# Expert 0's early rows moved from the first expert stage into the attention's plan, and expert 2's weights put behind the first transposes

## The chip, the cores and the metric

The kernel runs as one program on one core of a Trainium2 chip. The metric is the device time of one execution in microseconds (us). The engines are PE (TensorE, with PEld its weight loads), DVE (VectorE), ACT (ScalarE), POOL (GpSimd) and SP (SyncE, used here for DMA issues alone).

## The reference

Three stages follow each other; each takes the output of the one before.

```python
# 1: attention, 4 x 8 heads, 768 tokens, head size 48; one state (48x48) per head
y[t] = q[t] @ state
v_old = state^T k_n[t];  state += beta[t] * outer(k_n[t], v[t] - v_old)

# 2: x is (3072, 384); eight experts, each token to one of them
logits = x @ w_gate;  e_idx = argmax(logits);  probs = softmax(logits)
eom = sigmoid(x @ w_output_gate)
for e in range(8):
    rows = e_idx == e
    out[rows] = probs[rows, e] * eom[rows, e] * (relu(x[rows] @ w1[e]) @ w2[e])   # 384 -> 1024 -> 384

# 3: four experts, every token through all of them
p = domain_probs / domain_probs.sum(-1)
out = sum over e of p[:, e] * (relu(x @ w1[e]) @ w2[e])
```

## The kernel before

**Number formats.** Weights and rows are split into two f16 halves (a high part, and what is left, "lo"); one product is three f16 matmuls (high x high, high x lo, lo x high). One layer over a block of rows is 72 matmuls of 128x128 by as many columns as there are rows: 8 groups of 9 in the first layer (384 to 1024), 3 groups of 24 in the second (1024 to 384). Each group ends with two evictions: ACT writes the high half (L789, in the second layer L801), DVE the lo half (L790, L802).

**Stages.** Attention and routing come first (to about 311 us). The tokens are worked off in 12 chain steps of 64 tokens per sequence (L410); behind each step the finished tokens are transposed (L529, evicted to xT by ACT, L255), multiplied with both gates (L536), written to a table `xd` in DRAM, and counted by expert with prefix sums (L554, L570) into `run` and `acc`. After step 8, `early` (L587 to L600) takes the first 192 rows (EW) of experts 0 and 1 that are known by then, gathers them from `xd` by indirect DMAs into GZ, normalises them (`norm`, L578 to L583) and transposes them by DMA into `xe[0]` and `xe[1]`. `weights` loads the weights of experts 0 (into the buffer kq) and 1 (wa, wb) meanwhile. When all tokens are through, `counts` copies the counts and the row lists into `wid`.

The second stage, `moe1`, then works on windows of rows, one call of `window_` each: the early 192 rows of expert 0 (L787 with xe, L799), those of expert 1, the 240 other rows of expert 0, the 240 of expert 1, then 432 rows for each of experts 2 to 7. `fetch` gets what a window needs: indirect gathers on POOL (L774, xg<-xd,wid; four column buffers of 128 rows), `norm` through two buffers xh, transposes by DMA on SP (L732, xt<-xh; two buffers xt), and for experts 2 to 7 the weights, in seven DMAs on SP through three staging tiles s (L732), split into halves by ACT and DVE (L738, L739). Expert 2's weights go to the buffers w. Results go to `x2` in DRAM by three DMAs of POOL (L805, x<-y), one per 128 of the 384 outputs. `put` (L866, L867, eld<-EL) writes the scales of the rows. Rows beyond 432 of an expert are handled by a general loop that doesn't run here; the arithmetic that finds out (`spill`, recorded as L208) is strewn between.

The third stage, `moe2` (L928, L947), runs from 537.8 us to the end.

**What sets the order.** `Plan` simulates the engines: each operation has an engine, a modelled duration, what it reads and writes, and a priority (smaller is sooner); an engine takes the ready operation with the smallest priority, urgent ones (chain, evictions) first. The instructions are then issued in that order, so each engine runs a fixed list. Attention and routing are one plan, with four PSUM banks as a pool (`Lazy` takes one when the plan runs an operation with `take`); `moe1` is a second plan, with banks of its own, whose instructions all follow those of the first on each engine. Chain step n has priority n, so 20 comes behind all chain steps.

Of the kernel before, what the change touches and what calls it, by code (L numbers as in the profile page):

```python
# [72 lines left out]
STB = 3  # L73
XW = 408
# [408 lines left out]
class Router:  # L483

    NXR=4
    def __init__(self,ctx,tc,dp):
        self.tc=tc; self.nc=tc.nc; self.xd=dp.tile([N,XW],F32,name="xd"); self.eld=dp.tile([N+512,MW],F32,name="eld"); self.ord=dp.tile([NE*N+512,1],I32,name="ord")
# [109 lines left out]
    def weights(self,x):  # L597

        at=self.at; nc=self.nc; st=[(a,[('stw',j)]) for j,a in enumerate(at.stw)]; i=0; h=2*KD*FF
        for e,w,t in (((0,0,self.kq[:,0:h]),(0,1,self.kq[:,h:])),((1,0,self.wa),(1,1,self.wb)))[x]:  # L600
            kc=([('kqT',3-w,x,y) for x in range(2) for y in range(2)]+[('GQ',2,x,1-w) for x in range(2)]) if e else []; at.op('G',1,lambda: None,(),kc+[('Wc',e,w)],'claim')
            n,f,m=((KD,FF,512),(KF,DM,DM))[w]
            src=self.ahead[w][e].rearrange("(n p) f -> p n f",p=128); t=t.rearrange("p (l n f) -> p l n f",l=2,n=n); g=f"wl {2*e+w}"
            for a in range(n):
                for x in range(0,f,m):
                    s,ks=st[i%2]; i+=1; s=s[:,0:m]; at.prio=WPR; h_,l_=(t[:,j,a,x:x+m] for j in range(2)); k=[('W',e,w,a,x)]
                    at.dma(s,src[:,a,x:x+m],(),ks,g,xfer=m*1.42,q=WQ); at.prio=WPR+0.5
                    at.act(100+.833*m,h_,s,ks+[('Wc',e,w)],k,g,scale=64.0)
                    at.op(WLE,70+1.042*m,lambda s=s,h_=h_,l_=l_: nc.vector.scalar_tensor_tensor(out=l_,in0=s,scalar=64.0,in1=h_,op0=ALU.mult,op1=ALU.subtract),ks+k,[('W2',e,w,a,x)],g)
    def counts(self):  # L610
# [100 lines left out]
class Moe:  # L711
# [3 lines left out]
    def __init__(self,ctx,tc,r,w1,w2,v1,v2,out):  # L715
# [26 lines left out]
    def weight(self,t,key,src,n,width):  # L742
# [103 lines left out]
    def moe1(self):  # L846
        nc=self.nc; tc=self.tc; r=self.r; pl=self.pl=Plan(tc,HOP); self.si=self.xi=self.bi=self.ci=self.hi=self.yi=0; self.pp_=0; self.parts={}
        with ExitStack() as c:
# [22 lines left out]
            for e in range(NE):  # L871
# [116 lines left out]
def deltanet_moe(tc,q,k,v,beta,wg,wo,w1,w2,probs,v1,v2,out):  # L988
    nc=tc.nc
    with ExitStack() as ctx:  # L990
        dp=ctx.enter_context(tc.tile_pool(name="dp",bufs=1,space=DRAM))
        r=Router(ctx,tc,dp)
        with ExitStack() as c2:
# [3 lines left out]
            at.ahead=r.weights; r.setup(c2,at,plan,wg,wo,probs); r.ahead=(w1,w2); at.run(); r.counts()  # L997
# [31 lines left out]
```

## Time and profile before

| | us |
|---|---|
| Median of 3 runs | 1254.89 |
| Lowest and highest | 1251.54, 1254.93 |
| The profiled execution, its own time | 1257.36 |
| Its span | 1255.8 |
| PE busy in the span | 1179.4 (94%) |
| DVE, ACT, POOL busy | 781.1, 618.7, 640.4 |

The span is what the profiler recorded between the first and the last instruction; the execution's own time is 1.6 us more, and times of runs are to be compared with the own time. A share of busy time is a mean over stages with different limits, so the windows of the section of rows show the stretches around the change apart. A timeline row is a run of like instructions on an engine: when the first started, from there to the end of the last, how many there were (x), and in brackets the idle time of the engine ahead of it with what ended it; the rows of a longer question join differently from those of a shorter one. "SPq" or "POOLq" marks the DMA queue of an engine.

### The profile page before, as it was taken

Reading aid. Unit: us, or ns where it says so; the run is one execution under the profiler, and the core shown is the slowest. Engines: PE = TensorE matmul, PEld = TensorE weight load, DVE = VectorE, ACT = ScalarE, POOL = GpSimd, SP = SyncE. Lnnn points to the kernel's source line nnn. Section 1 sums busy time; section 2 is a strip of 40 time slices with the busy share of each in tenths; the row PEclk is TensorE's granted clock in tenths of the full one; section 3 lists DMA queues with packets and bytes.
Section 4 is the critical chain, followed back from the end, with each engine's and each line's share of the span. In section 5 each row is a group of like instructions: output and inputs, shape, how many; then the busy total and the mean of one; then the engine's idle time right before and its main releaser. Section 6 shows DMA issues by size and latency. Waiting matters only on the chain.

```text
span 1255.8 us, 38782 instructions
## 1 busy us (share of the span) xinstructions
PE 1179.4 (94%) x16595; PEld 1031.4 (82%) x16595; DVE 781.1 (62%) x1583; ACT 618.7 (49%) x1129; POOL 640.4 (51%) x896
## 2 busy tenths in 40 slices
PE   6988888877989999999999999999999999999997
PEld 5877777766974555589999999999999999999997
DVE  3766837664777787236666566677565776555555
ACT  4546664543545655235445444454444454444442
POOL 9643431442474350055665454576444675566565
PEclk9889998886999999999999999999999999999999
DMA  8445442324779976021111111111111220111101
GB/s 137 84 94 121 97 98 45 98 74 110 182 176 233 244 184 175 29 67 39 40 39 39 35 43 44 48 51 39 34 44 50 65 64 28 37 54 52 52 27 39
DMA packets 151457, 100.74 MB, mean 80 GB/s; under 512 B 107696, under 2 KB 140432, under 8 KB 151280
## 3 DMA queue, kind: packets, MB, share of 16 engines
q1 hardware_dynamic: 133520, 69.18, 22.4%
q0 software_dynamic: 9216, 23.50, 6.7%
q10 hardware_dynamic: 8544, 5.53, 1.5%
q8 instruction: 131, 2.15, 0.7%
q14 instruction: 46, 0.38, 0.1%
HBM read 77.09 MB, written 15.77 MB: 74 GB/s over the span
## 4 chain that ended last, share of the span: by engine, by line
PE 56%; DVE 0%; issue 0%; POOL 0%; ACT 0%; POOLq 0%
PE b L928 30%; PE b L947 26%; POOL out_dram L966 0%; DVE h L940 0%; DVE cc L958 0%; DVE wa L962 0%; DVE sm L958 0%; ACT h L939 0%; ACT a L930 0%; POOL sep L965 0%; POOLq L1024 0%; POOLq L966 0%
## 5 line engine op out<-in xcount | busy, mean ns | idle before, releaser
L928 PE MATMUL b<-wb,v 128*128 128x256 f16 x3456 | 392.6, 273 | 0.4 <-PEq L895 0.4
L928 PEld LDWEIGHTS <-v 128*128 128x128 f16 x3456 | 336.7, 98 | 37.8 <-issue 0.8
L947 PE MATMUL b<-v,h 128*128 128x192 f16 x4032 | 348.2, 246 | 0.0
L947 PEld LDWEIGHTS <-h 128*128 128x128 f16 x4032 | 335.5, 98 | 2.4 <-DVE h L940 0.2
L936 POOL TENSOR_TENSOR S<-a 128x256 f32<-128x256 f32 x192 | 150.8, 804 | 249.8 <-ACT a L930 249.5
L940 DVE TENSOR_TENSOR h<-a,h 128x768 f16<-128x768 f32 x96 | 132.6, 1381 | 134.8 <-ACT h L939 126.5
L940 DVE TENSOR_TENSOR h<-S,h 128x1024 f16<-128x1024 f32 x96 | 117.7, 1226 | 125.8 <-ACT h L939 125.6
L930 ACT ACTIVATE a<-b 128x512 f32<-128x512 f32 x192 | 113.8, 595 | 151.2 <-PE b L928 149.1
L939 ACT ACTIVATE h<-S 128x1024 f16<-128x1024 f32 x96 | 101.4, 1056 | 161.7 <-POOL S L936 142.1
L936 POOL TENSOR_TENSOR S<-S,a 128x256 f32<-128x256 f32 x96 | 126.9, 1322 | 0.0
L939 ACT ACTIVATE h<-a 128x768 f16<-128x768 f32 x96 | 80.9, 843 | 3.0
L936 POOL TENSOR_TENSOR S<-a,S 128x256 f32<-128x256 f32 x96 | 77.0, 802 | 7.2
L958 DVE TENSOR_TENSOR cc<-b,sm 128x192 f32<-128x192 f32 x192 | 58.5, 345 | 2.4 <-ACT sm L952 2.4
L789 ACT ACTIVATE h<-b 128x432 f16<-128x432 f32 (+2 forms) x80 | 35.7, 454 | 40.3 <-PE b L787 36.3
L805 POOL DMA_DIRECT2D x<-y x27 | 19.3, 721 | 68.9 <-DVE y L802 60.8
L790 DVE SCALAR_TENSOR_TENSOR h<-b,h 128x432 f16<-128x432 f32 (+2 forms) x80 | 40.7, 511 | 17.5 <-ACT h L789 17.1
L774 POOL DMA_INDIRECT xg<-xd,wid x28 | 30.2, 1077 | 38.7 <-DVE xh L583 22.0
L958 DVE TENSOR_TENSOR sm<-b,sm 128x192 f32<-128x192 f32 x144 | 46.2, 348 | 1.5
L799 PE MATMUL b<-h,kq 128*128 128x432 f16 (+2 forms) x288 | 42.4, 304 | 4.8 <-DVE h L790 4.8
L787 PE MATMUL b<-xt,w 128*128 128x432 f16 x216 | 42.1, 355 | 2.5 <-DVE wa L739 2.0
L739 DVE SCALAR_TENSOR_TENSOR v<-s,v 128x512 f16<-128x512 f32 (+2 forms) x56 | 41.6, 761 | 4.1 <-ACT v L738 3.9
L267 POOL DMA_DIRECT2D stw<-in_moe_w_dram x28 | 16.0, 571 | 52.6 <-DVE X L374 19.9
(279 smaller groups left out, 1748.0 us busy)
## 6 DMA issues: line engine op xcount, KB each, us to landing
wb<-x SPq DMA_DIRECT2D x72, 256.0 KB, 3.2
s<-in_moe_w_dram SPq DMA_DIRECT2D x40, 384.0 KB, 4.2
s<-in_moe_w_dram SPq DMA_DIRECT2D x18, 512.0 KB, 4.3
s<-in_moe_w_dram SPq DMA_DIRECT2D x24, 256.0 KB, 4.7
xd<-ys ACTq DMA_DIRECT2D x24, 192.0 KB, 3.1
x<-y POOLq DMA_DIRECT2D x18, 216.0 KB, 4.2
stw<-in_moe_w_dram POOLq DMA_DIRECT2D x12, 256.0 KB, 4.0
stw<-in_moe_w_dram POOLq DMA_DIRECT2D x16, 192.0 KB, 3.5
```

The costliest lines, as they stand in the source:

```text
L739: self.op('V',(150+1.042*n)*self.slow,lambda: self.nc.vector.scalar_tensor_tensor(out=lo,in0=s,scalar=64.0,in1=hi,op0=ALU.mult,op1=ALU.sub ...
L787: nc.tensor.matmul(out=ps,lhsT=w1[:,a,k,f*128:(f+1)*128],rhs=xt[:,b*KD+k],start=i==0,stop=i==8); i+=1
L789: self.op('A',160+.85*n,lambda ps=ps,h=h: nc.scalar.activation(out=h[:,0],in_=ps,func=AF.Relu),[('p1',pi)],[('h',hi,0)],**U)
L790: self.op('V',150+1.042*n,lambda ps=ps,h=h: nc.vector.scalar_tensor_tensor(out=h[:,1],in0=ps,scalar=0.0,in1=h[:,0],op0=ALU.max,op1=ALU.sub ...
L799: nc.tensor.matmul(out=ps,lhsT=w2[:,a,f,d*128:(d+1)*128],rhs=hs[f][0][:,b],start=(f,i)==(0,0),stop=(f,i)==(KF-1,2))
L928: for c,y in PASS: nc.tensor.matmul(out=F[k][:,f],lhsT=w[:,c,d,c_:c_+128],rhs=self.xk[B%2][d][:,y,256*i:256*i+256],start=(f,z)==(0,0),stop ...
L930: self.op('A',620,lambda k=k,g=g: A.activation(out=a[ja][:,g].rearrange("p x t -> p (x t)"),in_=F[k].rearrange("p a t -> p (a t)"),func=AF ...
L936: self.op('G',930,lambda o=o,x=x,y=y,w=w: G.tensor_tensor(out=X[o],in0=X[x],in1=X[y],op=w),ka,[ks])
L939: self.op('A',200+.833*m,lambda h=h,q=q,g=g: A.activation(out=h[:,0,:,q],in_=g,func=AF.Copy),kg,[kh+(0,)])
L940: self.op('V',1400 if m==768 else 1350,lambda h=h,q=q,g=g: V.tensor_tensor(out=h[:,1,:,q],in0=g,in1=h[:,0,:,q],op=ALU.subtract),kg+[kh+(0, ...
L947: for z,(c,d) in enumerate(PASS): nc.tensor.matmul(out=Q[k][:,o,0:192],lhsT=h[:,c,g,x],rhs=w[:,d,m,y],start=(m,o,z)==(0,0,0),stop=(m,z)==( ...
L958: self.op('V',340,lambda o=o,k=k,y=y,x=x: V.tensor_tensor(out=o,in0=Q[k][:,y,0:192],in1=s[:,x],op=ALU.add),[(qk,k),('sm',z,x)],[ko])
```

## The change

`Router.window(e)` is new. It is called once, for expert 0, ahead of `counts`, and so puts the early 192 rows of expert 0 through both layers inside the attention's plan, at priority 20 (EPR): the same 72 + 72 matmuls (L624 and L633 in the changed kernel), 11 evictions on ACT (L626, L635), 11 on DVE, and three DMAs on POOL to x2. Its h and y tiles lie in the buffers GQ of steps 3 and 4, its banks come from the pool of four. To write x2 there, its DRAM tiles are made in the router. In `moe1` the call of `window_` for these rows goes. And the weight DMAs of expert 2 now name the first transposed block, `('xt',0,0)`, as something they read, so the plan issues them no sooner than that is there. Behind the new function all line numbers are 28 larger, above it 2 larger.

```diff
--- before.py
+++ after.py
@@ -71,6 +71,8 @@
 AQ = 480
 XLO = 'V'
 STB = 3
+EPR = 20
+LTK = ('xt', 0, 0)
 XW = 408
 MW = 24
 RMQ = 'D'
@@ -484,7 +486,7 @@
 
     NXR=4
     def __init__(self,ctx,tc,dp):
-        self.tc=tc; self.nc=tc.nc; self.xd=dp.tile([N,XW],F32,name="xd"); self.eld=dp.tile([N+512,MW],F32,name="eld"); self.ord=dp.tile([NE*N+512,1],I32,name="ord")
+        self.tc=tc; self.nc=tc.nc; self.xd=dp.tile([N,XW],F32,name="xd"); self.eld=dp.tile([N+512,MW],F32,name="eld"); self.x2=[dp.tile([128,2,N+WIN],F16,name=f"x2{k}") for k in range(KD)]; self.ord=dp.tile([NE*N+512,1],I32,name="ord")
         c=self.c=ctx.enter_context(tc.tile_pool(name="rc",bufs=1)); T=lambda n,s,d=F32: c.tile(s,d,name=n)
         self.wgo=T("wgo",[128,KD,16])
         self.tri=T("tri",[128,128],F16); self.ones16=T("ones16",[128,128],F16)
@@ -607,6 +609,32 @@
                     at.dma(s,src[:,a,x:x+m],(),ks,g,xfer=m*1.42,q=WQ); at.prio=WPR+0.5
                     at.act(100+.833*m,h_,s,ks+[('Wc',e,w)],k,g,scale=64.0)
                     at.op(WLE,70+1.042*m,lambda s=s,h_=h_,l_=l_: nc.vector.scalar_tensor_tensor(out=l_,in0=s,scalar=64.0,in1=h_,op0=ALU.mult,op1=ALU.subtract),ks+k,[('W2',e,w,a,x)],g)
+    def window(self,e):
+
+        at=self.at; nc=self.nc; n=EW; t=f"ew {e}"; at.prio=EPR+0.1*e; w=[x.rearrange("p (l n f) -> p l n f",l=2,n=m) for x,m in zip(((self.kq[:,0:2*KD*FF],self.kq[:,2*KD*FF:]),(self.wa,self.wb))[e],(KD,KF))]
+        kw=[[(z,e,0,a,x) for z in ('W','W2') for a in range(KD) for x in range(0,FF,512)],[(z,e,1,a,0) for z in ('W','W2') for a in range(KF)]]
+        U=[x.rearrange("p h i -> p (h i)").bitcast(F16)[:,2*n*j:2*n*j+2*n].rearrange("p (a t) -> p a t",a=2) for i in (3,4) for x in at.GQ[i] for j in range(5)]; free=lambda s: [('GQ',3+s//10,hh,s//5%2) for hh in range(2)]
+        hs=U[0:8] if e==0 else U[8:16]; y0=16; s0=8*e; x=self.xe[e]; kx=[('xe',e,j) for j in range(2)]
+        def lo(q,k,o,reads,wr,give,op0,sc): at.op('V',150+1.042*n,lambda: nc.vector.scalar_tensor_tensor(out=o[:,1],in0=q(),scalar=sc,in1=o[:,0],op0=op0,op1=ALU.subtract),reads,wr,t,give=give)
+        for f in range(KF):
+            k=('ep',e,f); P=Lazy(at,k); h=hs[f]; kh=('eh',e,f)
+            def mm(P=P,f=f):
+                i=0
+                for d in range(KD):
+                    for a,b in ((0,0),(0,1),(1,0)): nc.tensor.matmul(out=P[:,0:n],lhsT=w[0][:,a,d,f*128:f*128+128],rhs=x[:,b*KD+d],start=i==0,stop=i==8); i+=1
+            at.op('P',9*(n/2.4+3),mm,kx+kw[0],[k],t,take=[k],lat=LP,ni=18)
+            at.op('A',160+.85*n,lambda P=P,h=h: nc.scalar.activation(out=h[:,0],in_=P[:,0:n],func=AF.Relu),[k],[kh+(0,)],t,after=free(s0+f))
+            lo(lambda P=P: P[:,0:n],k,h,[k,kh+(0,)],[kh+(1,)],[k],ALU.max,0.0)
+        for d in range(KD):
+            k=('eq',e,d); P=Lazy(at,k); y=U[y0+d]; ky=('ey',e,d)
+            for f0 in range(0,KF,2):
+                def mm(P=P,d=d,f0=f0):
+                    for f in (f0,f0+1):
+                        for i,(a,b) in enumerate(((0,0),(0,1),(1,0))): nc.tensor.matmul(out=P[:,0:n],lhsT=w[1][:,a,f,d*128:d*128+128],rhs=hs[f][:,b],start=(f,i)==(0,0),stop=(f,i)==(KF-1,2))
+                at.op('P',6*(n/2.4+3),mm,[('eh',e,f,j) for f in (f0,f0+1) for j in range(2)]+kw[1],[k],t,take=[k] if f0==0 else (),lat=LP,ni=12)
+            at.op('A',160+.85*n,lambda P=P,y=y: nc.scalar.activation(out=y[:,0],in_=P[:,0:n],func=AF.Copy,scale=2.0**-8),[k],[ky+(0,)],t,after=free(y0+d))
+            lo(lambda P=P: P[:,0:n],k,y,[k,ky+(0,)],[ky+(1,)],[k],ALU.mult,2.0**-8)
+            at.dma(self.x2[d][:,:,0:n],y,[ky+(0,),ky+(1,)],[('x2',d)],t,xfer=n*2,q='G')
     def counts(self):
         at=self.at; nc=self.nc; cp=Lazy(at,'wcnt')
         at.op('P',60,lambda: nc.tensor.matmul(out=cp[:,0:8],lhsT=self.ones16,rhs=self.run,start=True,stop=True),['run','rc'],['wcnt'],"cnt",take=['wcnt'])
@@ -721,9 +749,9 @@
 
         a=[t.bitcast(F32).rearrange("p (j d) -> p j d",d=DM) for t in (r.kq,r.wa)]; self.acc=lambda j: a[j//16][:,j%16]
         w=r.wb; self.xk=[[w[:,1024*(KD*i+k):1024*(KD*i+k)+1024].rearrange("p (y t) -> p y t",y=2) for k in range(KD)] for i in range(2)]
-        self.x2=[self.dp.tile([128,2,N+WIN],F16,name=f"x2{k}") for k in range(KD)]
+        self.x2=r.x2
         pp=ctx.enter_context(tc.tile_pool(name="pp",bufs=1,space=PSUM)); self.bank=[pp.tile([128,512],F32,name=f"b{i}") for i in range(8)]
-    gate=(); slow=1.0
+    gate=(); slow=1.0; late=()
     def op(self,e,dur,fn,reads=(),writes=(),**k):
         k.setdefault('prio',self.prio); self.pl.add(e,dur,fn,reads,writes,**k)
     def dma(self,out,in_,reads,writes,xfer,turn=False):
@@ -745,7 +773,7 @@
         v=src.rearrange("(n p) f -> p n f",p=128); self.claim(key)
         for a in range(0,n,step):
             m=step*width; s,k=self.stage(m)
-            self.dma(s.rearrange("p (n f) -> p n f",f=width),v[:,a:a+step],(),[k],m*WX)
+            self.dma(s.rearrange("p (n f) -> p n f",f=width),v[:,a:a+step],self.late,[k],m*WX)
             h,l=(t[:,j,a:a+step].rearrange("p n f -> p (n f)") for j in range(2))
             for x in range(0,m,m//2): self.pair(s[:,x:x+m//2],h[:,x:x+m//2],l[:,x:x+m//2],[k,key],key+(a,x))
         out=[key+(a,x,j) for a in range(0,n,step) for x in (0,m//2) for j in (0,1)]; self.parts.setdefault(key,set()).update(out); return out
@@ -856,7 +884,7 @@
             def fetch(e):
                 if e>=NE: return
                 i=B_[e]; self.prio=10*(e-1)-3; x=self.gather(wid[:,e],e,0 if e>1 else EW); self.prio=10*(e-2)+3 if e>2 else 2
-                t=[t.rearrange("p (l n f) -> p l n f",l=2,n=n) for t,n in zip(W[i],(KD,KF))]
+                t=[t.rearrange("p (l n f) -> p l n f",l=2,n=n) for t,n in zip(W[i],(KD,KF))]; self.late=[LTK] if e==2 else ()
                 kw=[self.weight(W[i][j],('W',i,j),self.w[j][e],n,f) for j,n,f in ((0,KD,FF),(1,KF,DM))] if e>1 else [[('W',i,0)],[('W',i,1)]]
                 ahead[e]=x,t,kw
             def colf(e):
@@ -876,7 +904,7 @@
                     if e==6: self.weight6(self.vw[0][1],('v',1,0),self.v[0][1],m)
                 if e==0:
                     colf(1); cols[0][0]=0; x1,t1,kw1=ahead[1]
-                    self.pp_=0; self.window_(0,*t,kw,(r.xe[0],[]),cols[0]); self.pp_=3; late=self.window_(1,*t1,kw1,(r.xe[1],[]),cols[1],ys=ye)
+                    self.pp_=3; late=self.window_(1,*t1,kw1,(r.xe[1],[]),cols[1],ys=ye)
                     self.pp_=6; put(0); self.window_(0,*t,kw,x,cols[0],EW); self.prio=10
                     for f in late: f()
                 else:
@@ -994,7 +1022,7 @@
             plan=Plan(tc,HOP)
             at=Attention(c2,tc,plan,q,k,v,beta,r.wa,r.wb,r.done)
             at.prio=0
-            at.ahead=r.weights; r.setup(c2,at,plan,wg,wo,probs); r.ahead=(w1,w2); at.run(); r.counts()
+            at.ahead=r.weights; r.setup(c2,at,plan,wg,wo,probs); r.ahead=(w1,w2); at.run(); r.window(0); r.counts()
             plan.emit()
         m=Moe(ctx,tc,r,w1,w2,v1,v2,out)
         m.moe1(); m.moe2()
```

The routing's tail, on ACT (L255 and L257 are the same evictions; xT are those of the transposed tokens, ys those of the chain, b banks of `moe1`). Before:

```order
L255 ACTIVATE w_135<-rw_145 128x384
L255 ACTIVATE xT<-pb_147 128x384
L255 ACTIVATE ys_138<-pb_150 128x4x2x48
L255 ACTIVATE ys_138<-pb_148 128x4x2x48
L267 DMA xd<-ys_138 128x384 x2
L255 ACTIVATE xT<-pb_149 128x384
L255 ACTIVATE xT<-pb_148 128x384
L789 ACTIVATE h_5746<-b_5729 128x192
```

In the changed kernel (GQ_114 and GQ_115 hold h, GQ_117 holds y, 128x192 are expert 0's early rows; h_5915 is the first of expert 1's early rows):

```order
L626 ACTIVATE GQ_114<-pb_153 128x192
L257 ACTIVATE xT<-pb_151 128x384
L626 ACTIVATE GQ_114<-pb_152 128x192
L626 ACTIVATE GQ_114<-pb_150 128x192
L626 ACTIVATE GQ_115<-pb_152 128x192
L257 ACTIVATE xT<-pb_153 128x384
L626 ACTIVATE GQ_115<-pb_151 128x192
L626 ACTIVATE GQ_115<-pb_150 128x192
L635 ACTIVATE GQ_117<-pb_151 128x192
L635 ACTIVATE GQ_117<-pb_153 128x192
L635 ACTIVATE GQ_117<-pb_152 128x192
L817 ACTIVATE h_5915<-b_5898 128x192
```

Of the eight evictions of the first layer two come earlier, among chain steps 10 and 11; the rows show one ahead of the last xT but one, three ahead of the last, two behind it, and then the three of the second layer, ahead of `moe1`. On PE the matmuls lie accordingly: 9 in chain step 10, 9 in step 11, the other 126 in groups of 9 and more between the tail's L529, L536, L554, L570 and L612.

The place where POOL passes from the routing (he, ha) to the first gathers (L774, in the changed kernel L802), with the waits of each instruction by the engine or DMA queue whose semaphore it needs. Before:

```order
L567 TENSOR_TENSOR ha<-he,iv 128x3x32 [waits PE_49]
L565 TENSOR_TENSOR he<-OH,oa_161 128x64 [waits DVE_49,Pool_49]
L567 TENSOR_TENSOR ha<-he,iv 128x2x32 [waits PE_49,Pool_49]
L567 TENSOR_TENSOR ha<-he,iv 128x2x32 [waits PE_49]
L774 DMA xg<-xd,wid 128x408 [waits DMAHW2_49,DMAHW3_49,DMAHW1_49,DMAHW4_49,DMAHW0_49,DMAHW5_49,DMASW6_49,DMAHW6_49,DMASW0_49,DMAHW7_49,DVE_49,Activation_49]
L774 DMA xg<-xd,wid 112x408
```

In the changed kernel (x_60 and x_61 are two of the three x2 tiles):

```order
L269 DMA x_59<-GQ_117 256x1x192 [waits DVE_49]
L567 TENSOR_TENSOR he<-OH,oa_164 128x64 [waits DVE_49,Pool_49]
L569 TENSOR_TENSOR ha<-he,iv 128x2x32 [waits PE_49,Pool_49]
L569 TENSOR_TENSOR ha<-he,iv 128x2x32 [waits PE_49]
L269 DMA x_60<-GQ_117 256x1x192 [waits DVE_49]
L269 DMA x_61<-GQ_117 256x1x192 [waits DMASW6_49,DVE_49]
L802 DMA xg<-xd,wid 128x408 [waits DMAHW2_49,DMAHW1_49,DMAHW3_49,DMAHW0_49,DMAHW4_49,DMASW6_49,DMAHW5_49,DMASW5_49,DMAHW6_49,DMASW4_49,DMAHW7_49,DMASW0_49,PE_49]
L802 DMA xg<-xd,wid 112x408
```

Two DMAs of expert 0's results now stand ahead of the first gather, which waits for DMASW4 to 6, the queues of the three results among them.

The same place on SP, from the last DMA of `xd` on (xt_5742 and xt_5911 are the first buffer of transposed rows, s the staging tiles of weights). Before:

```order
L267 DMA xd<-row 128x6x24
L732 DMA s_5763<-in_moe_w_dram 128x1024
L732 DMA s_5764<-in_moe_w_dram 128x1024
L732 DMA s_5765<-in_moe_w_dram 128x1024
L267 DMA xd<-row 128x2x24
L732 DMA s_5763<-in_moe_w_dram 128x2x384
L732 DMA s_5764<-in_moe_w_dram 128x2x384
L732 DMA s_5765<-in_moe_w_dram 128x2x384
L732 DMA_TRANSPOSE xt_5742<-xh 128x6x128
```

In the changed kernel:

```order
L269 DMA xd<-row 128x6x24
L269 DMA xd<-row 128x2x24
L760 DMA_TRANSPOSE xt_5911<-xh 128x6x128
L760 DMA_TRANSPOSE xt_5911<-xh 128x6x112
L760 DMA_TRANSPOSE xt_5912<-xh 128x6x128
L760 DMA_TRANSPOSE xt_5912<-xh 128x6x112
L760 DMA_TRANSPOSE xt_5911<-xh 128x6x128 x2
L760 DMA s_5932<-in_moe_w_dram 128x1024
L760 DMA s_5933<-in_moe_w_dram 128x1024
L760 DMA s_5934<-in_moe_w_dram 128x1024
L760 DMA_TRANSPOSE xt_5911<-xh 128x6x128
L760 DMA_TRANSPOSE xt_5911<-xh 128x6x48
```

Expert 2's weights stood ahead of all transposes, six of them; now the first six transposes stand ahead of the weights.

DVE in the rest of expert 0, which is 128x240 (L790, in the changed kernel L818; r<-ovt needs a result of POOL). Before:

```order
L802 SCALAR_TENSOR_TENSOR ye_5762<-b_5734,ye_5762 128x192
L208 SCALAR_TENSOR_TENSOR ovt_5786<-ovt_5786,off 128x1
L208 TENSOR_SCALAR val<-ovt_5786 128x8
L790 SCALAR_TENSOR_TENSOR h_5746<-b_5731,h_5746 128x240
L208 TENSOR_TENSOR r_5785<-ovt_5786,kw 128x64
L790 SCALAR_TENSOR_TENSOR h_5747<-b_5729,h_5747 128x240
L208 TENSOR_SCALAR r_5785<-r_5785 128x64
```

In the changed kernel:

```order
L818 SCALAR_TENSOR_TENSOR h_5917<-b_5898,h_5917 128x240
L585 SCALAR_TENSOR_TENSOR xh<-xg,sc,xh 112x384
L818 SCALAR_TENSOR_TENSOR h_5918<-b_5899,h_5918 128x240
L210 TENSOR_TENSOR ovt_5955<-few 128x1
L818 SCALAR_TENSOR_TENSOR h_5919<-b_5900,h_5919 128x240
L210 SCALAR_TENSOR_TENSOR ovt_5955<-ovt_5955,off 128x1
L210 TENSOR_SCALAR val<-ovt_5955 128x8
L818 SCALAR_TENSOR_TENSOR h_5920<-b_5898,h_5920 128x240
L210 TENSOR_TENSOR r_5954<-ovt_5955,kw 128x64
L210 TENSOR_SCALAR r_5954<-r_5954 128x64
```

Before, r<-ovt stood ahead of three of the eight h of expert 0's rest (h_5746 is the fifth of them). In the changed kernel these eight run from h_5923 through h_5920, so r<-ovt stands behind all of them.

## Rows read from the trace of the kernel before

**Rows 1.** Windows: us; busy of PE, PEld, DVE, ACT, POOL; clock; DMA; GB/s.

```profile
300.00:305.00 5.00, 4.42 (x59) 3.64 (x57) 1.66 (x10) 0.98 (x2) 0.00 (x0) 0.50 0.39 104
305.00:311.40 6.40, 2.49 (x33) 1.84 (x33) 5.24 (x29) 0.49 (x1) 3.51 (x9) 0.50 0.71 249
311.40:315.00 3.60, 3.57 (x26) 3.42 (x26) 0.97 (x7) 0.66 (x2) 1.37 (x2) 0.58 0.01 2
315.00:332.60 17.60, 16.84 (x205) 16.61 (x202) 14.50 (x40) 11.70 (x31) 11.13 (x28) 1.00 0.76 186
350.00:355.00 5.00, 3.37 (x17) 2.26 (x17) 4.46 (x15) 0.89 (x2) 3.80 (x11) 0.70 0.51 118
391.80:537.80 146.00, 145.00 (x794) 77.45 (x793) 95.50 (x215) 74.05 (x150) 42.95 (x62) 1.00 0.62 164
537.80:1255.80 718.00, 710.21 (x7488) 670.63 (x7488) 435.65 (x685) 334.12 (x493) 415.92 (x481) 1.00 0.15 45
```

**Rows 2.** PE timeline: start, us, instructions [idle before <-releaser].

```profile
296.51 0.54 PE L410 MATMUL rw<-r,C 32*32 32x48 f32 x32 [0.76 <-DVE EL L579]
311.43 7.54 PE L787 MATMUL b<-xe,kq 128*128 128x192 f16 x72 [0.28 <-DVE acc L573]
323.01 2.14 PE L799 MATMUL b<-h,kq 128*128 128x192 f16 x24
332.65 2.00 PE L787 MATMUL b<-xt,kq 128*128 128x240 f16 x18 [0.81 <-DMA xt<-xh]
351.13 0.47 PE L799 MATMUL b<-h,kq 128*128 128x240 f16 x3 [4.35 <-DVE h L790]
353.20 2.00 PE L787 MATMUL b<-xt,wa 128*128 128x240 f16 x9
357.66 1.09 PE L787 MATMUL b<-xt,wa 128*128 128x240 f16 x9
358.58 2.62 PE L799 MATMUL b<-h,kq 128*128 128x240 f16 x24
367.19 6.93 PE L799 MATMUL b<-h,wb 128*128 128x240 f16 x66
391.82 13.30 PE L799 MATMUL b<-h,w 128*128 128x432 f16 x72
```

**Rows 3.** POOL timeline, first gather, second half of a put, ovt.

```profile
313.33 1.00 POOL L774 DMA_INDIRECT xg<-xd,wid  x1 [2.47 <-issue]
346.71 0.79 POOL L867 DMA_DIRECT2D eld<-EL  x1 [7.43 <-issue]
350.07 0.43 POOL L208 TENSOR_SCALAR ovt<-cnt 128x64 f32<-128x64 f32 x1
```

**Rows 4.** DVE timeline, in expert 0's rest.

```profile
350.54 0.23 DVE L208 TENSOR_TENSOR r<-ovt,kw 128x64 f32<-128x64 f32 x1 [6.68 <-POOL ovt L208]
```

**Rows 5.** DMA issues from 311 to 395: KB each, median us to landing.

```profile
s<-in_moe_w_dram SPq DMA_DIRECT2D x9, 512.0 KB, 4.3
x<-y POOLq DMA_DIRECT2D x3, 96.0 KB, 3.9
xg<-xd,wid POOLq DMA_INDIRECT x16, 4.2
xt<-xh SPq DMA_TRANSPOSE x12, 4.3
eld<-EL POOLq DMA_DIRECT2D x2, 48.0 KB, 7.8
```

**Rows 6.** Groups by form, 288 to 392: busy us, mean ns | idle before.

```profile
L790 DVE SCALAR_TENSOR_TENSOR h<-b,h 128x192 f16<-128x192 f32 x16 | 5.6, 353 | 4.9 <-ACT h L789 4.9
L583 DVE SCALAR_TENSOR_TENSOR xh<-xg,sc,xh 128x384 f16<-128x384 f32 x8 | 5.1, 640 | 2.3 <-ACT xh L581 2.2
L789 ACT ACTIVATE h<-b 128x192 f16<-128x192 f32 x16 | 5.2, 329 | 11.4 <-PE b L787 11.2 <-ACT w L738 0.3
```

## The prediction

> **What bounds the kernel now.** I read the table of windows first: it says which stretches have slack for TensorE (PE). From 391.8 us to the end PE is busy 145.0 of 146.0 and 710.2 of 718.0 us [rows 1]: nothing there is waited for, and only what makes expert 2's second layer (391.82 [rows 2]) start earlier or later reaches the end. Ahead of it is a different picture: from 300 to 311.4, the routing's tail, PE works 4.42 + 2.49 = 6.9 of 11.4 us at a granted clock of 0.50, which is 1.2 GHz [rows 1]. The PE timeline, read second, shows what follows: expert 0's early rows from 311.43, expert 1's early rows, then at 332.65 the gathered rest of expert 0, with a pause of 4.35 us at 351.13 [rows 2].
>
> At the full clock one f16 matmul of 240 columns takes (6.93 - 2.62)/(66 - 24) = 0.103 us; those of 192 columns are cheaper in the ratio 2.14 to 2.62, 0.082 us; 72 of 432 columns take 13.30 [rows 2]. The work from 311.4 to 391.8 is therefore 288 x 0.082 + 288 x 0.103 + 13.3 = 66.5 of 80.4 us; 13.9 us go to pauses and half clock. The change takes 144 matmuls (11.8 us) out of this stretch and puts them into the attention's plan.
>
> **The routing's tail (A).** By the order of the changed kernel, 9 of the 144 stand in chain step 10 and 9 in step 11, where PE waits 0.76 us before the row at 296.51 [rows 2] (nine cost 9 x 0.082 = 0.74, so they fit or nearly; I charge 0.7 for both). The other 126 stand between the transposes and prefix sums of the tail: 126 x 0.082 = 10.3 us. The tail has 11.4 - 6.9 = 4.5 us free, so 5.8 must lengthen it. Two corrections: the first of them run at 1.2 GHz. The row at 311.43 took 7.54 us where 72 at full clock are 5.9 and the last one's own length of some 0.25: 1.4 lost until the clock rose, which the window at 311.4 shows as 0.58 and the next as 1.00 [rows 1, 2]. On the other hand the 6.9 us of old work would run faster once the clock is up; half would be 3.4, I take 2.0. Sum: 5.8 + 1.4 + 0.7 - 2.0 = 5.9, taken as +6. Bounds: +3.6 if the clock is up nearly all the time, +17.4 if all 126 and the old work run at 0.50 (126 x 0.165 + 6.9 = 27.7 from 301.1 on). The 11 evictions on ACT (0.33 each) and 11 on DVE (0.35) [rows 6] make 3.6 and 3.9 us on engines that are busy 1.5 and 6.9 of the 11.4 us [rows 1]; DVE, then at 10.8 of 17.4, has room, but an xT or a run can be late by one of them, which is inside the bounds.
>
> **From there to the rest of expert 0 (B).** Call T' the start of expert 1's early rows, 311.4 + 6. In the order, GpSimd's queue (POOL) now holds two of the three puts of expert 0's results right ahead of the first gather, and that gather waits for the landing of the last put. Before it started at 313.33 [rows 3], 1.9 after PE; now it comes one issue (0.9, as the other POOL issues near 1) and one landing later. The put of the same tile landed in 3.9 us, the put of L866 in 7.8 [rows 5]. I take 0.9 + 3.9 = 4.8 (lower bound 0, if that put is issued well before T'; upper 8.7). A figure of the Trainium skill, DMA: Bandwidth & Descriptors, section Anatomy of one DMA — SWDGE (gpsimd) path, would give less: its fit of 2.0 us and some 0.2 for the 96 KB; by it the sum would be 1.7 us better. The row of 3.9 for this very tile disagrees, and I go by the row.
>
> Gather to first matmul took 332.65 - 313.33 = 19.3 before [rows 2, 3]. Bare, it is 1.3 to the second gather, about 4.0 landing (row 4.2), 2.1 for the five steps of normalising (longest 0.64), some 0.5 between engines, 4.3 for a transpose to land: 12.2 [rows 5, 6]. The difference of 7 came from a DVE that was busy 14.5 of 17.6 us [rows 1] with weight halves of expert 2 and two experts' evictions. In the new order expert 2's weights stand behind six transposes on SP and expert 0's eight evictions are gone, so of the 7 I leave 2.3: 14.5, nearer to the bare 12.2. B = 4.8 + 14.5 = 19.3 after T'. Expert 1's early rows (144 x 0.082 = 11.8 us of PE) lie inside it even though the first eviction waits for the same landing and PE pauses some 3 us with three banks full. What hid the gathers before, two experts' early rows (21 us), now is one; that is where half of the gain goes: T' to the rest of expert 0 stays 19 us instead of the 11.8 of work in it.
>
> **Expert 0's and 1's rest (C).** 288 x 0.103 = 29.5. PE comes out of a pause, so it starts low: nine took 2.00 at 353.20 against 1.09 at 357.66 [rows 2], the granted clock around it being 0.70 [rows 1]; I take 1.6. Before, this part lasted from 332.65 to 374.12 (367.19 + 6.93), so 12.0 above the work. The 4.35 at 351.13 is named "DVE h", yet DVE sat in its queue at the r<-ovt of 350.54, idle 6.68 for POOL's ovt at 350.07 [rows 4, 3], and POOL stood behind L867 at 346.71, idle 7.43, which needs the landing of L866 (7.8) [rows 3, 5]. In the new order r<-ovt stands behind all eight h of expert 0's rest, so that stall goes; next late are two xh ahead of 2's transposes, which hold nothing of C. I leave 2.4 of the 12.0 beside the half clock: C = 33.5 (bounds 31.1, and 37.9 with the stall).
>
> **Expert 2's first layer (D).** 13.3 + 0.3. Its weights are now asked for behind six transposes, some 26 us after T' (first gathers landed at 4.8 + 1.3 + 4.0 = 10, then three pairs of rows through two buffers, each freed by the transpose before, 2.1 + 4.3 less overlap, say 5.3) instead of in the tail. Each of the seven transfers lands in 4.3 to 5 us, three at a time [rows 5]; the first layer's three would be in by T' + 36 with their halves split, and PE wants them at T' + 52.8. This cover of some 17 us is why I cost the later loading at nothing; without it each us late is a us lost.
>
> **Sum.** T' + 19.3 + 33.5 + 13.6 = 311.4 + 6 + 66.4 = 383.8 against 391.8: -8.0 us. From there on PE's order is unchanged; weight halves come about one expert later to DVE and ACT, but these have 50 us free in 146 [rows 1]. The profiled execution's own time of 1257.36 becomes 1249.4; the median shown is 2.47 lower than it, so 1254.89 - 8.0 = 1246.9, predicted as 1247.
>
> **The rivals.** Changes under 0.3% (3.8 us) cannot be told from none here.
> 1. The clock stays up in the tail: the new groups keep PE at 2.4 GHz, A is +3.6 and the put is issued before T'. For it: the clock rises within 3.6 us of dense work at 311.4; against: it stood at 0.50 in 300 to 305 with PE busy 4.42 of 5. Gain 8.0 + 2.4 + up to 3: about 1243.
> 2. The gathers or expert 2's weights take the gain. The put lands like L866 (7.8 instead of 3.9), and the ovt stall, or weights that come late, cost another 0 to 4.35: 1247 + 3.9 to 8.2, that is 1251 to 1255; 1252.5 as its time. For it: both waits hang on POOL's DMAs, whose landings in the rows scatter by 2; against: expert 2's weights no longer crowd them.
> 3. Slower: the tail runs at 1.2 GHz throughout. The groups are split by short f32 matmuls, and this very stretch shows 0.50 with PE busy. Then A is +17.4 in place of +6: -8.0 + 11.4 = +3.4, 1258.3. The break-even is A = +14, that is a granted clock of (126 x 0.082 + 6.9 x 0.50)/(10.3 + 14) = 0.57 between 300 us and T'; below it this case decides.
>
> **How the numbers follow.** Forecast 0.48 (own range 1244 to 1250, from put and chain being 3 off), rival 1 0.14, rival 2 0.23, rival 3 0.15. Faster takes the forecast and rival 1: 0.62; same is rival 2 but for a little: 0.22; slower rival 3 with that little: 0.16. Leaving out half of rival 1's far side and the far side of rival 3 gives 1242 to 1258.
>
> **What would show it.** In the changed profile: the new L624 and L633 rows of PE between 300 us and T', with the granted clock of that window (A); T' near 317.4; the first gather (L802) about 4.8 us after T', and idle until a put has landed; PE's pauses ahead of and in expert 1's early rows; expert 0's rest near T' + 19.3 (B); no pause of 4 us ended by DVE h in it (C); no idle time on expert 2's first layer for its weights (D); PE busy unchanged from expert 2's second layer on. The prediction is wrong if T' is beyond 322, if the rest of expert 0 begins later than T' + 24, or if PE gets pauses after expert 2 that it did not have.

## The result, and the profile after

| | us |
|---|---|
| Changed kernel, median of 4 runs | 1235.39 (1235.26 to 1237.38) |
| Before, median of 4 runs on the same occasion | 1253.22 (1250.63 to 1254.93) |
| Ratio | 0.9863, interval 0.9839 to 0.9887 |
| Profiled execution, own time and span | 1235.26, 1233.7 |

It is 17.8 us faster; 8 were forecast, and the time lies under the range of 1242 to 1258. On two later occasions the changed kernel had 1238.81 (4 runs, ratio 0.9878, 0.9840 to 0.9916) and 1239.99 (10 runs, 0.9906, 0.9876 to 0.9936), 13.2 and 11.6 us under before. Before spread from 1245.06 to 1260.73 over all its runs.

The windows of the changed kernel, columns as in [rows 1]:

```profile
288.00:294.00 6.00, 6.00 (x147) 5.49 (x144) 2.97 (x13) 3.18 (x9) 0.00 (x0) 1.00 0.29 68
294.00:300.00 6.00, 6.00 (x94) 5.75 (x92) 4.42 (x18) 2.53 (x8) 2.33 (x6) 1.00 0.21 51
300.00:306.10 6.10, 5.38 (x76) 5.28 (x73) 3.49 (x21) 0.99 (x3) 2.56 (x6) 1.00 0.09 20
306.10:324.20 18.10, 12.74 (x144) 11.87 (x144) 7.88 (x34) 4.28 (x13) 9.72 (x28) 1.00 0.40 101
324.20:355.30 31.10, 29.84 (x288) 28.18 (x289) 22.21 (x66) 16.37 (x39) 21.30 (x43) 1.00 0.77 183
355.30:368.80 13.50, 13.32 (x75) 7.06 (x74) 9.88 (x27) 8.49 (x18) 10.01 (x17) 1.00 1.04 261
368.80:514.80 146.00, 144.87 (x792) 77.35 (x791) 110.13 (x239) 84.07 (x173) 44.71 (x64) 1.00 0.75 199
514.80:1233.70 718.90, 710.49 (x7491) 670.72 (x7488) 436.29 (x685) 334.41 (x493) 417.51 (x481) 1.00 0.15 45
```

From 288 to 306 us PE is nearly filled, and the clock is 1.00 in each window: the tail that stood at 0.50 [rows 1] is gone. From 306.1 to 324.2 PE works 12.74 of 18.10 us; there the gathers are waited for. The last two windows are those of before to a microsecond.

Rows of PE's timeline of the changed kernel, from the last large group of chain step 11 to expert 2's second layer:

```profile
289.92 2.07 PE L412 MATMUL pb<-w,GQ 64*64 64x48 f32 x64
306.14 2.40 PE L815 MATMUL b<-xe,wa 128*128 128x192 f16 x27 [0.76 <-DVE GQ L618]
310.08 3.87 PE L815 MATMUL b<-xe,wa 128*128 128x192 f16 x45 [1.54 <-DVE h L818]
324.22 7.55 PE L815 MATMUL b<-xt,kq 128*128 128x240 f16 x72 [2.78 <-DMA xt<-xh]
343.70 1.08 PE L815 MATMUL b<-xt,wa 128*128 128x240 f16 x9 [0.86 <-DVE h L818]
348.55 6.93 PE L827 MATMUL b<-h,wb 128*128 128x240 f16 x66
355.31 5.09 PE L815 MATMUL b<-xt,w 128*128 128x432 f16 x27
360.58 8.37 PE L815 MATMUL b<-xt,w 128*128 128x432 f16 x45 [0.18 <-DVE h L818]
368.79 13.30 PE L827 MATMUL b<-h,w 128*128 128x432 f16 x72
```

In the kernel before, the first of these groups (64 small f32 matmuls) ran at half the clock, and expert 2's first layer had pauses:

```profile
297.49 3.65 PE L410 MATMUL pb<-w,GQ 64*64 64x48 f32 x64
373.95 5.09 PE L787 MATMUL b<-xt,w 128*128 128x432 f16 x27
385.12 6.86 PE L787 MATMUL b<-xt,w 128*128 128x432 f16 x27 [1.98 <-DVE wa L739]
```

I count from this group, because the part ahead of it is unchanged in nearly all of its order and yet differs by chance: in the fourteen traces of all kernels its start lies anywhere from 289.2 to 297.8 us, with other drops of the clock each time. The count leaves out 18 of the 144 matmuls, which stand ahead of it, in waits of some 0.75 us each; by the starts of the rows around them they cost about 0.5 us together (an estimate from the changed kernel's trace and the second one of before), so the gain counted from the group is too large by about that. The first profile of before had the second latest start, 297.49; the changed kernel's first had 289.92. Of the 22.1 us between the two spans 7.6 are this, and only 14.5 the change:

| from that group, us | before | forecast | after |
|---|---|---|---|
| to T' (before: to expert 0's early rows) | 13.9 | 19.9 | 16.2 |
| T' to the rest of expert 0 (before: two experts' early rows) | 21.2 | 19.3 | 18.1 |
| to expert 2's first layer | 41.3 | 33.5 | 31.1 |
| that layer | 17.9 | 13.6 | 13.5 |
| second layer of expert 2 to the end | 863.9 | 863.9 | 864.9 |
| sum | 958.3 | 950.2 | 943.7 |

(The forecast's +6 is put whole into the first line. The 41.3 of before hold 60 matmuls of expert 1's early rows, 4.9 us of work, which in the changed kernel come ahead of the rest of expert 0.) POOL's timeline of the changed kernel, the last put, the first gather and the second half of a later put:

```profile
306.38 0.68 POOL L269 DMA_DIRECT2D x<-GQ  x1 [0.58 <-DVE GQ L618]
309.54 1.03 POOL L802 DMA_INDIRECT xg<-xd,wid  x1 [2.48 <-PE b L815]
330.49 0.81 POOL L895 DMA_DIRECT2D eld<-EL  x1 [3.96 <-DVE h L818]
```

DVE's, its first instruction behind the put, and r<-ovt:

```profile
308.93 0.06 DVE L210 MEMSET off<- 128x1 f32 x1 [2.84 <-DMA x<-GQ]
334.32 0.23 DVE L210 TENSOR_TENSOR r<-ovt,kw 128x64 f32<-128x64 f32 x1 [1.70 <-issue]
```

The last put is issued at 306.38, and DVE, whose new tile needs its landing, goes on at 308.93: 2.5 us. The first gather follows at 309.54, 3.4 after T'. The profile names a matmul (b, L815) as what ended the gather's wait, but those matmuls ended at 308.54; that it was the landing is tested below (e8). r<-ovt at 334.32 has no wait on POOL any more (against 6.68 [rows 4]), and PE no pause above 0.9 us in the rest of the two experts (4.35 before [rows 2]); L895 still stands idle for 3.96 at 330.49, but nothing of PE is behind it.

### The profile page after: what moved, and what is told of

It is laid out like the page before. It is cut to its first block, busy times and chain, and to the rows that moved or that the text cites. A ratio compares the mean times of both kernels' runs of the same rounds, so it can differ in the third digit from the quotient of the medians.

```text
span 1233.7 us, 38757 instructions
## 1 busy us (share of the span) xinstructions
PE 1163.3 (94%) x16595; PEld 1018.3 (83%) x16595; DVE 778.2 (63%) x1583; ACT 619.2 (50%) x1129; POOL 642.0 (52%) x896
## 4 chain that ended last, share of the span: by engine, by line
PE 57%; DVE 0%; issue 0%; POOL 0%; ACT 0%; POOLq 0%
PE b L956 31%; PE b L975 26%; POOL out_dram L994 0%; DVE h L968 0%; DVE cc L986 0%; DVE wa L990 0%; DVE sm L986 0%; ACT h L967 0%; ACT a L958 0%; POOLq L1052 0%; POOL sep L993 0%; POOLq L994 0%
## 5 line engine op out<-in xcount | busy, mean ns | idle before, releaser
L818 DVE SCALAR_TENSOR_TENSOR h<-b,h 128x432 f16<-128x432 f32 (+2 forms) x72 | 37.8, 527 | 16.3 <-ACT h L817 16.2
L817 ACT ACTIVATE h<-b 128x432 f16<-128x432 f32 (+2 forms) x72 | 32.9, 466 | 29.5 <-PE b L815 29.0
L802 POOL DMA_INDIRECT xg<-xd,wid x28 | 30.5, 1088 | 22.8 <-issue 6.6
L269 POOL DMA_DIRECT2D stw<-in_moe_w_dram x28 | 16.0, 572 | 47.8 <-DVE X L376 17.9
L815 PE MATMUL b<-xt,w 128*128 128x432 f16 x216 | 40.2, 346 | 0.2 <-DVE h L818 0.2
L827 PE MATMUL b<-h,w 128*128 128x432 f16 x216 | 39.9, 346 | 0.0
```

Of the source, the lines that this page charges most:

```text
L815: nc.tensor.matmul(out=ps,lhsT=w1[:,a,k,f*128:(f+1)*128],rhs=xt[:,b*KD+k],start=i==0,stop=i==8); i+=1
L817: self.op('A',160+.85*n,lambda ps=ps,h=h: nc.scalar.activation(out=h[:,0],in_=ps,func=AF.Relu),[('p1',pi)],[('h',hi,0)],**U)
L818: self.op('V',150+1.042*n,lambda ps=ps,h=h: nc.vector.scalar_tensor_tensor(out=h[:,1],in0=ps,scalar=0.0,in1=h[:,0],op0=ALU.max,op1=ALU.sub ...
L827: nc.tensor.matmul(out=ps,lhsT=w2[:,a,f,d*128:(d+1)*128],rhs=hs[f][0][:,b],start=(f,i)==(0,0),stop=(f,i)==(KF-1,2))
```

## The experiments

Theory 1: the tail's low clock is due to its thin work, and the early rows, put there, keep PE at 2.4 GHz and so cost little. Rivals: the delay of expert 2's weights makes the gain (theory 2); or the clock in the tail is chance.

"From the group" below is the time from that group of chain step 11 to the end of the span, in one trace of each kernel; it leaves out the chance of the attention, which the times of the runs hold. "Tail" is the time from that group to the first matmul of the expert stage; in e3 it ends where expert 0's early rows begin, behind the routing. The expectations count the tail from an earlier group, 18.6 us before (from 292.85) and 20.2 in the changed kernel (from 285.95). Their "18.6 us at 0.50" is not what the trace shows: the mean over these 18.6 us is 0.62, since the clock fell only at 297.4.

| | median of runs, us (number) | before beside it | ratio, interval | tail, us | from the group |
|---|---|---|---|---|---|
| first part alone (e1) | 1249.55 (10) | 1251.43 | 0.9978, 0.9959 to 0.9996 | 16.2 | 951.5 |
| the same again (e10) | 1246.80 (1) | 1251.63 | | 16.4 | 951.9 |
| second part alone (e2) | 1247.54 (10) | 1251.43 | 0.9958, 0.9931 to 0.9986 | 12.7 | 953.4 |
| early rows behind the tail (e3) | 1247.20 (10) | 1251.43 | 0.9970, 0.9946 to 0.9993 | 12.6 | 954.7 |
| before + 144 thrown away (e4) | 1246.31 (4) | 1251.43 | 0.9940, 0.9920 to 0.9960 | 15.9 | 955.1 |
| before + 45 thrown away (e5) | 1248.12 (10) | 1252.04 | 0.9970, 0.9945 to 0.9995 | 12.2 | 954.6 |
| before + 144 + second part (e9) | 1247.74 (10) | 1252.04 | 0.9977, 0.9946 to 1.0008 | 15.9 | 952.4 |
| before again (e6) | 1255.10 (1) | 1251.63 | | 13.0 | 958.7 |
| after again (e7) | 1238.81 (4) | 1252.04 | 0.9878, 0.9840 to 0.9916 | 16.2 | 945.9 |
| after, third time (e11) | 1239.99 (10) | 1251.63 | 0.9906, 0.9876 to 0.9936 | 16.2 | 942.5 |
| y in xe (e8) | 1239.10 (6) | 1252.04 | 0.9871, 0.9841 to 0.9902 | 16.2 | 942.3 |
| the same again (e12) | 1236.42 (6) | 1251.63 | 0.9854, 0.9806 to 0.9903 | 16.2 | 941.0 |

**Does work in the tail hold the clock up?** Before, with 144 matmuls whose result is thrown away:

```diff
+ for g in range(16):   # dummy(16); 9 matmuls of expert 0's first layer each
+     at.op('P',9*(EW/2.4+3),mm,kw,[k],t,take=[k],lat=LP,ni=18)
+     at.op('V',80,lambda P=P: nc.vector.tensor_copy(out=self.dz,in_=P[:,0:8]),[k],['dz'],t,give=[k])
- at.run(); r.counts()
+ at.run(); r.dummy(16); r.counts()
```

> The kernel before with 144 added matmuls of 192 columns in the attention's plan at priority 20, in groups of 9 whose result is thrown away (one small DVE copy each); expert 0's early rows are still computed in the expert stage. It adds 11.9 us of work and moves none. Theory 1: the added matmuls raise the clock, the tail is 19.5 to 21 us at about 1.00 in place of 18.6 at 0.50, the expert stage starts at full clock (1.4 less), so the time is -2 to +3 us against before. Rival (the clock in the tail is chance, or set by the f32 work): they run at 0.50, the tail takes 26 us or more, +7 us or more.

The tail as one window (columns as in [rows 1]), first in the kernel before:

```profile
297.49:311.43 13.94, 9.42 (x134) 8.00 (x134) 7.44 (x40) 2.62 (x6) 3.51 (x9) 0.50 0.53 163
```

In the changed kernel:

```profile
289.92:306.14 16.22, 15.46 (x260) 15.02 (x260) 9.63 (x46) 5.41 (x15) 4.89 (x11) 1.00 0.22 51
```

In the second trace of the kernel before (e6):

```profile
294.81:307.81 13.00, 6.78 (x134) 5.51 (x134) 7.56 (x40) 2.62 (x6) 3.44 (x9) 0.74 0.57 175
```

With the 144:

```profile
292.80:308.73 15.93, 15.46 (x260) 15.04 (x261) 7.92 (x52) 2.58 (x6) 3.71 (x9) 1.00 0.47 144
```

126 of the added matmuls lie in this window, 10.3 us at full clock and 20.8 at half. The window grew by 2.0 and 2.9 us, at a clock of 1.00: the rival (26 us or more) is out. Compared with e6 the idle time went from 6.2 to 0.5 us, and the old work got shorter, 15.5 - 10.3 = 5 in place of 6.8 (9.4 where the whole window was at 0.50). By the runs the kernel is 5.1 us under before, outside the -2 to +3 that were expected. That it became faster with useless work is not the tail's doing: its window is longer, and the gain of 3 us from the group on lies from the rest of expert 0 to expert 2's second layer (53.1 us against 59.2). Of these 6 us 3.5 to 4.7 lie in expert 2's first layer, which took 17.9 us before (16.7 in e6) and here runs without a pause:

```profile
371.21 13.30 PE L798 MATMUL b<-xt,w 128*128 128x432 f16 x72
```

One of the pauses that went was for weight halves (1.98 <-DVE wa L739 at 385.12 above), so that expert 2's weights, asked for in the tail, come earlier against PE is a likely reason, but not shown.

The same with fewer:

```diff
- r.dummy(16)
+ r.dummy(5)
```

> The kernel before with 45 added matmuls of 192 columns (3.7 us) in place of 144, all of them in chain step 11 and ahead of the tail's last transpose; results thrown away. Theory 1 (filled PE keeps the clock up): the clock stays at 1.00 as long as they last and falls in the thinner rest of the tail or not at all; about 2 to 8 us under before. Rival (only a tail filled to its end, or work taken out of the expert stage, pays): no change, or 1 to 4 us over before.

27 of the 45 lie in the window:

```profile
289.20:301.36 12.16, 8.40 (x161) 7.55 (x161) 7.38 (x44) 2.58 (x6) 3.38 (x9) 0.86 0.62 187
```

They cost nothing: 12.2 us against 13.0 to 13.9, and by the runs the kernel is 3.9 us under before, within what theory 1 expected. In this trace the clock falls at 298.0, after the end of the last of them at 294.4, and stays low to 304.8: the work held the clock only where it stood. In the four traces whose tail has no added work (before, e6, e2, e3) there is a stretch at 1.2 GHz in the tail, in the nine with added work to its end (after, e7, e11, e8, e12, e1, e10, e4, e9) none. That is too regular for chance.

The kernel before, without an edit:

> The kernel before itself, for a second trace. If its first profile was an unlucky one in the unchanged part (its last PE work of chain step 10 came 2 to 8 us later than in the seven other traces): the same place lies at 265 to 270 us, the tail has a stretch at 1.2 GHz again (theory 1), from chain step 11's last large group to expert 0's early rows it takes 12.5 to 14 us, and the pause of 4 us ended by DVE h in expert 0's rest is there again. If the tail's low clock was chance, it is at 1.00 here.

The low clock is there again, and the sum from the group agrees to 0.4 us; the group itself starts 2.7 us earlier than in the first trace, inside the spread. The pause in expert 0's rest is there too:

```profile
349.48 0.76 PE L799 MATMUL b<-h,kq 128*128 128x240 f16 x3 [4.82 <-DVE h L790]
```

**The place in the tail.** The same code, but the early rows wait for the row lists:

```diff
- kx=[('xe',e,j) for j in range(2)]
+ kx=[('xe',e,j) for j in range(2)]+['wid']
- at.run(); r.window(0); r.counts()
+ at.run(); r.counts(); r.window(0)
```

> The changed kernel, but expert 0's early rows wait for the row lists wid, so all 144 matmuls come behind the routing's tail and none in it; SP's order is that of the changed kernel. Theory 1: the tail is as before, 18.6 us at 0.50, the gathers come some 15 us after it, behind the puts, and the time is within 4 us of before. If the place in the tail did not matter (rival: the gain is from the weights and the stall of 4.35 us alone), it would be within 4 us of the changed kernel.

```profile
292.79:305.34 12.55, 7.08 (x135) 5.82 (x134) 6.69 (x34) 2.62 (x6) 3.12 (x9) 0.69 0.24 56
305.34:319.41 14.07, 13.26 (x148) 12.97 (x148) 4.30 (x13) 3.63 (x11) 1.54 (x2) 0.91 0.04 10
```

The tail is as in the other traces without added work, 12.55 us at 0.69, and the early rows take 14.07 us behind it. From the group on it is 8.8 to 12.2 us slower than the changed kernel's three traces, with SP's order the same: that is what the place is worth, most of the 11.8 us of PE work that was moved. By the runs it is 4.2 us under before, just outside the 4 that were expected, and 7.2 to 8.4 over the changed kernel's medians of the two later occasions.

**The two parts alone.** The first is the changed kernel less its second part (e1, e10), the second the kernel before with it (e2):

```diff
 e1, e10:
- self.late=[LTK] if e==2 else ()
+ self.late=()
 e2:
- self.dma(s.rearrange("p (n f) -> p n f",f=width),v[:,a:a+step],(),[k],m*WX)
+ self.dma(s.rearrange("p (n f) -> p n f",f=width),v[:,a:a+step],self.late,[k],m*WX)
```

> The changed kernel without its second part: expert 2's weights are again asked for ahead of the transposes. If the gain comes from the routing's tail running at the full clock with the early rows in it (theory 1), the tail keeps the 20.2 us and the clock of 1.00 of the changed kernel, the rest of expert 0 starts up to 5 us later after T' because DVE is busy with weights again, and the time is 10 to 15 us under before. If the delay of the weights makes most of the gain (theory 2), it is less than 5 us under before.

> The kernel before with the second part alone: expert 2's weights behind the first transposes, expert 0's early rows left in the expert stage. Theory 1 (clock in the tail): a granted clock of 0.50 in the tail as before, a gain of 2 to 6 us from gathers that no longer share DVE and the DMA queues with weights. Theory 2 (the weights): 12 us or more under before.

The tails are as theory 1 says, 16.2 us at 1.00 with the early rows, and for the second part alone:

```profile
293.09:305.79 12.70, 6.92 (x134) 5.65 (x134) 7.49 (x40) 2.62 (x6) 3.52 (x9) 0.72 0.24 56
```

From the group on the first part is worth 6.8 us, the second 4.9, both 12.4 to 15.8 (three traces): they add up, with 1 to 4 more. By the runs they do not: 1.9 and 3.9 us alone, 11.6 to 17.8 together, so each part seems to need the other. Neither "the weights make the gain" nor my "10 to 15 from the first" held. In its trace the second part alone brings expert 2's second layer 9.9 us closer to the group and loses 5.0 behind it: there PE waits 5.0 us for h (DVE, L790), and 0.6 in the kernel before. What the first part lacks stands in one row, ahead of the rest of expert 0:

```profile
329.60 9.12 PE L815 MATMUL b<-xt,kq 128*128 128x240 f16 x72 [7.27 <-DMA xt<-xh]
```

There PE idles 7.27 us for the transposes (2.78 in the changed kernel), and the clock is at 1.2 GHz from about 326 to 333. The runs of e1, with a median 1.9 us under before, show a smaller gain than its trace (6.8), so it was traced again:

> The kernel with the early rows in the tail but without the delay of expert 2's weights, again. Its first trace was its fastest run of ten (1244.72; median 1249.55). If the weights ahead of the transposes cost time by the wait for the transposed rows: a pause of 5 us or more ended by DMA xt ahead of the rest of expert 0 (7.27 in the first trace), with a drop of the clock behind it, and up to 5 us more than then. If the spread comes from the attention alone, the stretch from T' to expert 2's second layer is again 68.4 us.

```profile
332.34 9.21 PE L815 MATMUL b<-xt,kq 128*128 128x240 f16 x72 [8.08 <-DMA xt<-xh]
```

The pause is there again, 8.08, the sum from the group agrees to 0.4 us, and from T' to expert 2's second layer it takes 68.6 us, as against 68.4. That speaks for the attention as the source of the spread, with two traces. Why its runs gain less than the traces stays open; each trace is one execution, and among the ten runs the first, profiled one was the fastest.

Both edits, `dummy(16)` and that of e2, in the kernel before (e9):

> The kernel before with both: the 144 thrown-away matmuls in the tail and expert 2's weights behind the first transposes; expert 0's early rows stay in the expert stage. If the two parts of the change add up apart from the 11.9 us of early rows that moved, this is the changed kernel plus about 8 to 12 us: 1243 to 1247. If the two parts need each other only because both keep PE's clock up, most of the changed kernel's gain shows here: 1238 to 1243.

1247.74, just above the upper end of 1243 to 1247, and 952.4 from the group on, 6.5 to 9.9 over the changed kernel: with the early rows still in the expert stage most of its gain is not there. It is the moved work, and not the clock alone.

The changed kernel twice more, without an edit:

> The changed kernel itself, to have its times and its trace again on this chip. If the gain is real and not a lucky state of the clock in the unchanged part ahead of chain step 10: about 1235 us, 14 to 18 under before, tail 16 to 17 us from chain step 11's last large group at a clock of 1.00. If it was luck: 1240 or more, with a spread as wide as the one of before (10 us).

> The changed kernel, on the same chip as the next one. 1235 to 1240 us, from T' to the rest of expert 0 about 18.0 us.

The times were 1238.8 and 1240.0, up to 1241.9 and 1246.2, with tails of 16.22 each. They lie between what I had expected of a real gain (1235) and of luck (1240 or more): the gain is real, 11.6 to 13.2 us here, and the 1235.4 of the first four runs was partly luck.

**The put's landing (step B).** The results of the early rows are kept in xe:

```diff
- y=U[y0+d]; ky=('ey',e,d)
+ y=self.xe[e][:,2*d:2*d+2]; ky=('ey',e,d)
- [ky+(0,)],t,after=free(y0+d))
+ [ky+(0,)],t,after=kx)
```

> The changed kernel with the results y of expert 0's early rows kept in the buffer xe of these rows, which the expert stage does not reuse. The first gather and the first eviction of expert 1's early rows then wait for no landing of a put; PE's and SP's orders are unchanged. By step B the gathers come up to 3.2 us earlier (309.54 against the last put's issue at 306.38) and the pauses of 1.54 and part of 2.78 us ahead of the rest of expert 0 go: 2 to 4 us under the changed kernel. If the gather is held by something else (the prefix's xd rows, POOL's queue), no change.

> The changed kernel with the early rows' results in xe, on the same chip as the one before it in this list. If the 2.2 us by which the rest of expert 0 came earlier after T' reach the end: 1 to 3 us under it, from T' to the rest of expert 0 about 15.8 us. If they are given back later or lost in the spread of the attention's clock: within 1 us.

POOL of e8, the last put ahead of the gathers, the first gather, and the third put:

```profile
312.96 0.73 POOL L269 DMA_DIRECT2D x<-xe  x1
314.48 1.03 POOL L802 DMA_INDIRECT xg<-xd,wid  x1 [0.79 <-DVE off L210]
319.29 0.76 POOL L269 DMA_DIRECT2D x<-xe  x1
```

PE of e8, expert 1's early rows and the rest of expert 0:

```profile
314.03 3.89 PE L815 MATMUL b<-xe,wa 128*128 128x192 f16 x45 [0.76 <-DVE off L210]
329.80 5.40 PE L815 MATMUL b<-xt,kq 128*128 128x240 f16 x51 [1.15 <-DMA xt<-xh]
```

The gather starts 0.45 us after T' in place of 3.4, and the rest of expert 0 after 15.8 us (15.2 in e12) in place of 18.1. The edit changed POOL's order too: the third put now stands behind the four gathers. Its issue took 0.7 us ahead of them, so most of the 3.0, but not all, is the landing, and DVE's wait of 2.84 for it is gone. So the wait was where step B put it. At the end nothing is shown: from the group on 942.3 and 941.0 against 942.5 to 945.9; by the runs 1239.10 against 1238.81 on one occasion and 1236.42 against 1239.99 on the other, with overlapping intervals. The 2 to 4 us that I expected of e8 did not come.

## Why the prediction was wrong

**A was mis-sized, and by its clock.** I charged 5.9, taken as +6, for the tail. It grew by 2.3 us (16.2 against 13.9), or 3.2 against the second trace of before; against e3, with SP's order of the changed kernel, by 3.7. The charge that failed against every trace is "the first of them run at 1.2 GHz": 1.4 lost. From the first of the tail's added groups to the last the clock was at 1.00. The 0.7 for the 18 matmuls lie ahead of this stretch.

How the rest of A splits depends on the trace of before. Against the first, 3.8 of the 4.5 us of idle time were used up, and of the old work I gave back 2.0 for a higher clock where 9.4 became 5.1, 4.3 us. But 1.6 of these 4.3 lie in one group (3.65 against 2.07) that I had not counted into the tail, and it took 2.07 in the second trace of before as well: that much is chance and not the change. Against the second, 5.5 us of idle time were used up, and the higher clock gave 1.7.

The rival that I gave 0.14 had the clock right, and its +3.6 lies near the 2.3 to 3.7. Its other half, a put issued before T', did not come (306.38, T' at 306.14). That the row of 300 to 305 showed 0.50 with PE busy 4.42 of 5 misled me: it was busy in part because it was slow (twelve matmuls of L536 took 0.83 us there, and 0.53 at 295.23).

**B was 1.2 too long.** The put landed in 2.5 us, not 3.9: the row [rows 5] comes from a stretch with the DMA engines 0.76 busy [rows 1], and here they were 0.40; that the load makes the difference is not shown. The figure that I had set aside, an estimate of some 2.2 by the Trainium skill, DMA: Bandwidth & Descriptors, section Anatomy of one DMA — SWDGE (gpsimd) path, was nearer. Gather to first matmul was 14.7 us, 14.5 had been taken between 12.2 and 19.3.

**C was 2.4 too long, D right.** The stall of 4.35 went as the order said. The half clock behind the pause did not come in the changed kernel's first trace (in e7 it did, for 3.4 us), and 1.6 us of waits were left over the 29.5 of work. The 12.0 "above the work" from which I left 2.4 was misread: it held the 4.9 us of expert 1's early rows. That r<-ovt caused the stall was not isolated. But each trace with the order of before in this place has it (before, e6, e4 and e5, 2.5 to 4.8 us), and in e2 and e9, where r<-ovt stands behind seven of the eight h, there is none.

**The rest.** I took later weight halves at nothing; 0.9 us was lost (2.6 in e7, none in e11); expert 2's weights were in time. In the traces the errors add up: 3.7 in A, 1.2 in B, 2.4 in C and 0.1 in D, less 0.9, are the 6.5 us between 8.0 and 14.5. The base was high too, and that is chance: 1254.89 of three runs, where on four occasions the medians of before were 1251.4 to 1253.2. From 1252 the traces give 1252 - 14.5 = 1237.5, between the measured 1235.4 and 1240.0.

## What to carry to other kernels

Filling a thin stretch of TensorE can cost far less than the work put in, here 2.3 to 3.7 us for 10.3: it uses the gaps, and it speeds up what was there if the granted clock was at 1.2 GHz. Price a stretch at 0.50 by what like rows take at the other level, here 3.65 us for 64 matmuls of a kind of which 32 took 1.08 at 287.18 in the same trace. Take a landing time from a stretch as loaded as the one you forecast: 3.9 us was read where the DMA engines were busy, 2.5 was found where they were less so.

## What had not been expected of the hardware

144 useless matmuls in a thin stretch made the kernel no slower (0.9940, 0.9920 to 0.9960). The attention, all but unchanged, differs by up to 8.6 us from trace to trace, with drops of the clock at other places in each; a single profile of either kernel is no base for a difference of this size until both are counted from a common row. Even then it is one execution: e1 gained 6.8 us by its trace and 1.9 by its ten runs.
